# First features of xA issued on ScalarE's queue, and the softmax's 1e-9 as an addend of its sum

## The chip, the cores and the metric

The kernel runs on one core of a Trainium2 chip. The metric is the device time of one execution in microseconds (us). The engines are TensorE (PE, with its weight loads as PEld), VectorE (DVE), ScalarE (ACT), GpSimd (POOL) and SyncE (SP). SP and ACT can both issue DMA transfers; their issues appear as SPq and ACTq.

## The reference

The input x has 8 x 4096 tokens of 192 features. Eight heads of 24 features each have 7 taps; the taps go through a softmax with a small guard, and a causal convolution over the last 7 tokens follows. Its output goes through a dense layer to 2048, a squared ReLU with a scale and a bias, and a dense layer back to 192.

```python
w = np.exp(weight - np.max(weight, axis=-1, keepdims=True))
w = w / (np.sum(w, axis=-1, keepdims=True) + 1e-09)
x_pad = np.concatenate([np.zeros((B, pad, D)), x], axis=1)
idx = np.arange(S)[:, None] + np.arange(K)[None, :]
x_unf = x_pad[:, idx, :].reshape(B, S, K, H, group)
out = np.einsum('hk,bskhg->bshg', w, x_unf)        # then reshaped to tokens x 192
h = out @ w_in
g = s * np.maximum(h, 0.0) ** 2 + b
return g @ w_out
```

## The kernel before

Features lie on the partitions and tokens along the free axis. The 192 features are cut into A, the first 128, and B, the last 64, of which two blocks of 512 tokens are laid on top of each other so that B too fills 128 partitions. A step n takes 1024 tokens, that is two blocks j; there are 32 steps. The hidden 2048 are 8 pairs p of 2 x 128. Matrices are split into a high and a low fp32r part, and products are formed as high x high, high x low and low x high.

`Tokens.load` brings the tokens of a step: it clears the six padding columns of xA where a sequence begins (L133, on POOL), then issues xB (L135) and xA (L138) on SP. At n = 0 only the first 512 tokens of xA go with L138; then come the first third of the words of pair 0 (`fetch`, L338) and the rest of xA (L141).

The setup lies at the end of the pools: the taps' DMA (L345), `tok[0].load()`, an identity made on POOL, an Exp on ACT whose result nobody reads (L357; it has the activation table loaded early), and the softmax of the taps on DVE and ACT, L358 to L366: maximum, subtraction, Exp, sum, addition of 1e-9, reciprocal, product. More words and the two scalars follow on SP's queue.

`head` then does step 0's convolution: PE warms up on a tile of zeros (L382) and convolves both blocks of B at once into a PSUM tile with seven diagonal matrices that ACT makes from the taps (L390, L245); DVE convolves block 0 of A (L149 for the first tap, L151 for the six others); PE convolves block 1 of A (L245 again). Splits follow: ACT casts the sum to the high part (L166, L215), and the low part is a subtraction on DVE (L168) or, for the sums in PSUM, a matmul with minus the identity (L218) and a copy (L219). Weight words are split on ACT and DVE at L292 to L325. The first matmuls of the dense layer are at L526.

The order of DVE, ACT and PE is the order of the program text (`in_order`), and so is that of SP's queue in `head`. The rest is ordered by the recording layer, with the waits that data need; `behind(...)` holds an instruction back until the engine's last one so far has been issued.

Of the kernel before, what the change touches and what calls it, by code (L numbers as in the profile page):

```python
# [9 lines left out]
F32 = mybir.dt.float32  # L10
# [3 lines left out]
AF = mybir.ActivationFunctionType  # L14
ALU = mybir.AluOpType
AX = mybir.AxisListType

P = 128
# [17 lines left out]
def conv_attention_then_squared_relu_mlp(  # L36
# [23 lines left out]
    nc = tc.nc  # L60
    D, T = outT.shape
    NPAIR = weights64.shape[0]
    K = taps.shape[2]
    PAD = K - 1
# [5 lines left out]
    const = ctx.enter_context(tc.tile_pool(name="const", bufs=1))  # L70
# [10 lines left out]
    def last_of(*engines):  # L81


        traced = nc.cur_bb.bb.instructions
        last = [next(i for i in reversed(traced) if i.engine == e.engine) for e in engines]

        @contextmanager
        def context():
            with ExitStack() as stack:
                for i in last:  # L90
                    stack.enter_context(tc.issue_after(i))
                yield

        return context

    def behind(*engines):
        return last_of(*engines)()
# [20 lines left out]
    class Tokens:  # L118
# [7 lines left out]
        def load(self):  # L126
            n = self.n
            t0 = n * SUP
            self.xA = xin.tile([P, PAD + SUP], F32, name="xA")
            self.xB = xin.tile([P, PAD + BLK], F32, name="xB")  # L130
            skip = PAD if t0 % seq == 0 else 0
            if skip:
                nc.gpsimd.memset(self.xA[:, 0:PAD], 0.0)  # L133

            nc.sync.dma_start(self.xB, xB[n])  # L135
            x0 = t0 - PAD
            cut = PAD + BLK if n == 0 else PAD + SUP
            nc.sync.dma_start(self.xA[:, skip:cut], xA[:, x0 + skip : x0 + cut])  # L138
            if n == 0:
                fetch(0, 0, CI)  # L140
                nc.sync.dma_start(self.xA[:, cut:], xA[:, BLK:SUP])  # L141
# [192 lines left out]
    def fetch(p, a=0, z=None):  # L334
        if a == 0:
            words[p] = wordp.tile([P, CT, 2], I32, name="words")
        z = z or CT
        nc.sync.dma_start(  # L338
            words[p][:, a:z].rearrange("p f w -> p (f w)"), w_words[p, :, 2 * a : 2 * z]
        )  # L340

    idle = act.tile([P, 2, BLK], F32, name="q")[:, 0, 0:P]
    nc.gpsimd.memset(idle, 0.0)
    tap = const.tile([P, 2, K], F32, name="tap")
# [9 lines left out]
    tmax = const.tile([P, 2], F32, name="tmax")  # L354
    tsum = const.tile([P, 2], F32, name="tsum")

    nc.scalar.activation(tsum, idle[:, 0:2], AF.Exp)  # L357
    nc.vector.reduce_max(tmax, tap, axis=AX.X)  # L358
    nc.vector.tensor_tensor(
        tap, tap, tmax.unsqueeze(2).to_broadcast([P, 2, K]), op=ALU.subtract  # L360
    )
    nc.scalar.activation(tap, tap, AF.Exp)
    nc.vector.reduce_sum(tsum, tap, axis=AX.X)
    nc.vector.tensor_scalar(tsum, tsum, 1e-9, None, op0=ALU.add)
    nc.vector.reciprocal(tsum, tsum)
    nc.vector.tensor_tensor(tap, tap, tsum.unsqueeze(2).to_broadcast([P, 2, K]), op=ALU.mult)  # L366

    fetch(0, CI, CT)
    fetch(1)
# [474 lines left out]
```

## Time and profile before

| | us |
|---|---|
| median of 3 runs (2297.73 to 2298.25) | 2298.07 |
| the profiled execution | 2297.88 |
| its span, first to last instruction | 2296.1 |
| PE busy | 2289.9 |
| DVE busy | 1755.8 |
| ACT busy | 1287.5 |
| POOL busy | 317.0 |

The span is what the trace covers; the profiled execution's own time is 1.8 us longer. A row of the timeline gives the start from the span's beginning, the duration, the engine, the line of the kernel, the operation, output<-input, and in brackets how long the engine sat idle before it and what ended that. A DMA's issue is short; the time to its landing stands in the rows on DMA issues.

### The profile page before, as it was taken

The page shows a single profiled execution, that of the slowest core. Times are in us where ns is not written, and L with a number is a line of the kernel's source. Part 1 is how long each engine was busy: PE and PEld are TensorE (multiplying, and loading weights), DVE is VectorE, ACT ScalarE, POOL GpSimd, SP SyncE. Part 2 cuts the span into 40 slices and gives each one's busy share as a digit, 9 for nine tenths or more (in the row PEclk, how much of TensorE's full clock was granted, in tenths as well). Part 3 has the DMA queues.
Part 4 walks back from the last instruction along what each step waited for, and adds up shares of the span by engine and source line. Part 5 has one row for each costly group of instructions (what it writes and reads, how often), then busy time and mean ns, then how long its engine had stood idle before and what let it go on. Part 6 is the DMA issues. An engine that isn't in the chain of part 4 may idle for free.

```text
span 2296.1 us, 45081 instructions
## 1 busy us (share of the span) xinstructions
PE 2289.9 (100%) x19330; PEld 1829.1 (80%) x19330; DVE 1755.8 (76%) x1995; ACT 1287.5 (56%) x1410; POOL 317.0 (14%) x205
## 2 busy tenths in 40 slices
PE   9999999999999999999999999999999999999999
PEld 6788888888888888888888888888888888888887
DVE  8898777777777787777877777777777777777764
ACT  8755555555555556455555555555555555555554
POOL 0021101101111011110110111101101111011110
PEclk9999999999999999999999999999999999999999
DMA  5113112121121111111111212112121121111110
GB/s 175 38 40 86 42 38 61 49 54 42 43 56 51 51 42 50 49 52 52 44 49 47 55 49 53 47 40 60 49 54 43 43 56 51 51 43 43 42 38 17
DMA packets 46168, 117.51 MB, mean 51 GB/s; under 512 B 7760, under 2 KB 8016, under 8 KB 45968
## 3 DMA queue, kind: packets, MB, share of 16 engines
q1 hardware_dynamic: 45824, 114.50, 18.9%
q8 instruction: 151, 2.47, 0.5%
q14 instruction: 49, 0.40, 0.1%
q10 hardware_dynamic: 144, 0.13, 0.0%
HBM read 31.64 MB, written 25.17 MB: 25 GB/s over the span
## 4 chain that ended last, share of the span: by engine, by line
PE 99%; DVE 1%; DMA 0%; ACT 0%; SPq 0%; issue 0%; DVEq 0%
PE acc L609 50%; PE h L526 47%; PE acc L571 0%; PE acc L572 0%; PE acc L577 0%; PE acc L576 0%; PE acc L578 0%; DVE accA L151 0%; DMA xA<-in_xA 0%; DVE t L303 0%; DVE t L300 0%; DVE t L296 0%; DVE oB L671 0%; ACT W L310 0%; PE acc L668 0%
## 5 line engine op out<-in xcount | busy, mean ns | idle before, releaser
L540 ACT ACTIVATE q<-h 128x1024 f32<-128x1024 f32 x512 | 526.3, 1028 | 966.0 <-PE h L526 958.8
L549 DVE CAST qh<-q 128x1024 fp32r<-128x1024 f32 x497 | 372.8, 750 | 455.6 <-ACT q L547 454.6
L554 DVE TENSOR_TENSOR ql<-q,qh 128x1024 fp32r<-128x1024 f32 x512 | 656.7, 1283 | 56.9 <-ACT qh L549 3.3
L609 PE MATMUL acc<-qh,W 64*128 64x512 f32 x3960 | 622.0, 392 | 0.0
L547 ACT ACTIVATE q<-q 128x1024 f32<-128x1024 f32 x512 | 543.0, 1061 | 16.0
L609 PEld LDWEIGHTS acc<-qh,W 64*128 64x128 f32 x3960 | 370.9, 184 | 91.1
L526 PE MATMUL h<-sA,W 64*128 64x512 f32 x3072 | 441.8, 392 | 0.0
L526 PE MATMUL h<-wA,W 64*128 64x512 f32 x3072 | 441.2, 392 | 0.0
L526 PE MATMUL h<-tB,W 64*128 64x512 f32 x1536 | 439.6, 392 | 0.0
L526 PE MATMUL h<-wB,W 64*128 64x512 f32 x1536 | 439.6, 392 | 0.0
L609 PE MATMUL acc<-ql,WB 64*128 64x512 f32 x1980 | 391.2, 392 | 0.0
L609 PE MATMUL acc<-qh,WB 64*128 64x512 f32 x1980 | 391.1, 392 | 0.0
L609 PE MATMUL acc<-ql,W 64*128 64x512 f32 x1980 | 391.0, 392 | 0.0
L633 POOL TENSOR_TENSOR oB<-oB,oB 128x512 f32<-128x512 f32 x61 | 115.4, 1892 | 1731.7 <-ACT oB L632 1731.7
L151 DVE SCALAR_TENSOR_TENSOR accA<-xA,tap,accA 128x512 f32<-128x512 f32 x378 | 340.5, 901 | 6.8
L526 PEld LDWEIGHTS h<-sA,W 64*128 64x128 f32 x3072 | 287.3, 184 | 72.7 <-issue 1.5
L526 PEld LDWEIGHTS h<-wA,W 64*128 64x128 f32 x3072 | 287.7, 184 | 70.6
L526 PEld LDWEIGHTS h<-tB,W 64*128 64x128 f32 x1536 | 282.6, 184 | 47.1 <-issue 0.2
L526 PEld LDWEIGHTS h<-wB,W 64*128 64x128 f32 x1536 | 282.6, 184 | 23.7
L609 PEld LDWEIGHTS acc<-ql,WB 64*128 64x128 f32 x1980 | 185.5, 184 | 46.0 <-DVE ql L554 0.6
L609 PEld LDWEIGHTS acc<-ql,W 64*128 64x128 f32 x1980 | 185.5, 184 | 45.5
L609 PEld LDWEIGHTS acc<-qh,WB 64*128 64x128 f32 x1980 | 185.5, 184 | 45.4
(115 smaller groups left out, 1035.6 us busy)
## 6 DMA issues: line engine op xcount, KB each, us to landing
wA<-sA SPq DMA_DIRECT2D x126, 256.0 KB, 3.7
outT<-oA SPq DMA_DIRECT2D x63, 256.0 KB, 2.0
wB<-tB SPq DMA_DIRECT2D x60, 256.0 KB, 3.5
xA<-in_xA SPq DMA_DIRECT2D x24, 515.0 KB, 3.6
xB<-in_xB SPq DMA_DIRECT2D x32, 259.0 KB, 2.7
oC<-oB SPq DMA_DIRECT2D x61, 128.0 KB, 2.2
outT<-oC SPq DMA_DIRECT2D x60, 128.0 KB, 2.3
words<-in_w SPq DMA_DIRECT2D x7, 768.0 KB, 6.0
```

The source lines that it names most:

```text
L151: nc.vector.scalar_tensor_tensor(acc, src, w[:, k : k + 1], acc, op0=ALU.mult, op1=ALU.add)
L526: nc.tensor.matmul(h[:, i, :], w_in(w, p, chunk[0], rows), chunk[part], start=start, stop=stop)
L540: nc.scalar.activation(q, h, AF.Relu)
L547: nc.scalar.activation(q, q, AF.Square)
L549: cast(qh, q)
L554: nc.vector.tensor_tensor(ql, q, qh.bitcast(F32), op=ALU.subtract)
L609: nc.tensor.matmul(accs[to + 2 * i], w(f, r), q[r, f % 2, :], start=start and f == 0, stop=stop and f == ends[i],)
L633: nc.gpsimd.tensor_tensor(o[1], o[1], o[3], op=ALU.add)
```

## The change

At step 0 the first 512 tokens of xA are issued by ACT instead of SP, and POOL's memset of the padding covers eight columns instead of six, so that it overlaps the first two columns that the transfer writes. The unread Exp is held behind ACT's last instruction so far, which is that issue. In the softmax the Exp writes into a new tile `powers` of 8 columns per group, whose last column POOL sets to 1e-9; the sum runs over all eight, the separate addition is gone, and the product reads `powers`. Line numbers grow by 4 to 9.

```diff
             if skip:
-                nc.gpsimd.memset(self.xA[:, 0:PAD], 0.0)
-
+                nc.gpsimd.memset(self.xA[:, 0 : PAD + 2 * (n == 0)], 0.0)
             nc.sync.dma_start(self.xB, xB[n])
             x0 = t0 - PAD
             cut = PAD + BLK if n == 0 else PAD + SUP
-            nc.sync.dma_start(self.xA[:, skip:cut], xA[:, x0 + skip : x0 + cut])
+            (nc.sync if n else nc.scalar).dma_start(
+                self.xA[:, skip:cut], xA[:, x0 + skip : x0 + cut]
+            )
...
-    nc.scalar.activation(tsum, idle[:, 0:2], AF.Exp)
+    with behind(nc.scalar):
+        nc.scalar.activation(tsum, idle[:, 0:2], AF.Exp)
...
-    nc.scalar.activation(tap, tap, AF.Exp)
-    nc.vector.reduce_sum(tsum, tap, axis=AX.X)
-    nc.vector.tensor_scalar(tsum, tsum, 1e-9, None, op0=ALU.add)
+
+    powers = const.tile([P, 2, K + 1], F32, name="powers")
+    nc.gpsimd.memset(powers[:, :, K:], 1e-9)
+    nc.scalar.activation(powers[:, :, 0:K], tap, AF.Exp)
+    nc.vector.reduce_sum(tsum, powers, axis=AX.X)
     nc.vector.reciprocal(tsum, tsum)
-    nc.vector.tensor_tensor(tap, tap, tsum.unsqueeze(2).to_broadcast([P, 2, K]), op=ALU.mult)
+    nc.vector.tensor_tensor(
+        tap, powers[:, :, 0:K], tsum.unsqueeze(2).to_broadcast([P, 2, K]), op=ALU.mult
+    )
```

SP's queue before, from the program's beginning (tap: the taps; words: weight words; DMAHW is a DMA's semaphore):

```order
L345 DMA tap<-in_taps 128x14
L135 DMA xB<-in_xB 128x518
L138 DMA xA<-in_xA 128x512
L338 DMA words<-in_w 128x768
L141 DMA xA<-in_xA 128x512
L338 DMA words<-in_w 128x768
L338 DMA words<-in_w 128x1536
```

SP's queue in the changed kernel, the same place:

```order
L349 DMA tap<-in_taps 128x14
L137 DMA xB<-in_xB 128x518
L342 DMA words<-in_w 128x768
L145 DMA xA<-in_xA 128x512
L342 DMA words<-in_w 128x768
L342 DMA words<-in_w 128x1536
```

The third issue, the first part of xA, is gone, and all behind it stand one place further ahead.

ACT before, from its first instruction (q: at L357 the tile of zeros, at L390 a diagonal):

```order
L357 ACT_TABLE_LOAD
L357 ACTIVATE tsum<-q 128x2 [waits Pool_49]
L362 ACTIVATE tap<-tap 128x14 [waits DVE_49]
L390 ACTIVATE q<-q,tap 128x128 [waits DVE_49,Pool_49]
L390 ACTIVATE q<-q,tap 128x128 x6
```

ACT in the changed kernel, the same place:

```order
L140 DMA xA<-in_xA 128x512 [waits Pool_49]
L362 ACT_TABLE_LOAD
L362 ACTIVATE tsum<-q 128x2
L370 ACTIVATE powers<-tap 128x2x7 [waits DVE_49]
L399 ACTIVATE q<-q,tap 128x128 [waits DVE_49,Pool_49]
L399 ACTIVATE q<-q,tap 128x128 x6
```

The issue of xA is now ACT's first instruction and waits for POOL; the table load and the unread Exp come behind it.

## Rows read from the trace of the kernel before

**Rows 1.** The page's first part: engine, busy us, share of the span, instructions.
```profile
PE 2289.9 (100%) x19330; PEld 1829.1 (80%) x19330; DVE 1755.8 (76%) x1995; ACT 1287.5 (56%) x1410; POOL 317.0 (14%) x205
```
**Rows 2.** Waits of PE, whole run: tile, line, releaser, us, times, longest.
```profile
PE acc L382 <- POOL xA L133: 1.0, 1, 1.0
PE acc L218 <- ACT sA L215: 0.4, 1, 0.4
PE acc L218 <- ACT hiB L215: 0.2, 1, 0.2
```
**Rows 3.** The chain of waits, 0 to 60 us: start us, us, what.
```profile
0.74 0.40 SPq L345
...
1.19 0.42 SPq L135
...
1.65 3.26 DMA xA<-in_xA
...
18.16 0.49 ACT sA L215
...
18.70 0.50 PE acc L218
```
**Rows 4.** Timeline, 0 to 16 us, ACT, SP, DVE: start, us, instruction, [idle before <-releaser].
```profile
0.73 1.28 ACT L357 ACT_TABLE_LOAD   x1 [0.73 <-PEq L834]
...
2.13 0.43 SPq L338 DMA_DIRECT2D words<-in_w  x1
...
2.79 0.21 ACT L362 ACTIVATE tap<-tap 128x14 f32<-128x14 f32 x1 [0.57 <-DVE tap L359]
...
3.04 0.17 DVE L363 TENSOR_REDUCE tsum<-tap 128x2 f32<-128x14 f32 x1 [0.28 <-ACT tap L362]
...
3.24 0.17 DVE L364 TENSOR_SCALAR tsum<-tsum 128x2 f32<-128x2 f32 x1
...
3.65 0.17 DVE L366 TENSOR_TENSOR tap<-tap,tsum 128x14 f32<-128x14 f32 x1
3.92 2.15 ACT L390 ACTIVATE q<-q,tap 128x128 f32<-128x128 f32 x7 [0.91 <-DVE tap L366]
...
5.05 0.49 DVE L149 TENSOR_SCALAR accA<-xA,tap 128x512 f32<-128x512 f32 x1 [1.23 <-DMA xA<-in_xA]
```
**Rows 5.** Timeline, the memset of xA's padding on POOL.
```profile
0.87 0.10 POOL L133 MEMSET xA<- 128x6 f32 x1
```
**Rows 6.** Timeline, PE from its first matmul to 18.70 us.
```profile
0.99 3.43 PE L382 MATMUL acc<-q 128*128 128x512 f32 x6 [0.99 <-POOL xA L133]
...
4.38 6.28 PE L245 MATMUL acc<-xB,q 128*128 128x512 f32 x14
...
10.49 1.88 PE L245 MATMUL acc<-xA,q 128*128 128x512 f32 x4
...
12.60 0.50 PE L218 MATMUL acc<-hiB,minus 128*128 128x512 f32 x1 [0.23 <-ACT hiB L215]
...
18.70 0.50 PE L218 MATMUL acc<-sA,minus 128*128 128x512 f32 x1 [0.40 <-ACT sA L215]
```
**Rows 7.** DMA issues of 1.5 to 2.4 us: queue, count, KB each, us to landing.
```profile
xB<-in_xB SPq DMA_DIRECT2D x1, 259.0 KB, 2.9
xA<-in_xA SPq DMA_DIRECT2D x1, 256.0 KB, 3.3
...
words<-in_w SPq DMA_DIRECT2D x1, 384.0 KB, 4.2
```
**Rows 8.** Stretches: busy us (instructions) by engine; PE clock, DMA share, GB/s.
```profile
2.50:3.00 0.50, 0.50 (x2) 0.14 (x1) 0.23 (x2) 0.20 (x1) 0.00 (x0) 1.00 0.83 153
3.00:3.50 0.50, 0.50 (x3) 0.41 (x2) 0.39 (x3) 0.01 (x1) 0.00 (x0) 1.00 0.99 282
...
0.00:20.00 20.00, 18.37 (x50) 8.55 (x52) 15.41 (x32) 14.93 (x35) 0.88 (x8) 1.00 0.59 187
```
**Rows 9.** Timeline near the end: the one DMA issue on ACT's queue.
```profile
2292.20 0.38 ACTq L690 DMA_DIRECT2D outT<-oA  x1
```

## Prediction

> **What bounds the kernel now.** I read the engine totals first: TensorE (PE) is busy 2289.9 of 2296.1 us [rows 1]. So the kernel is one long stream of matmuls, and a change can move the end only by moving the moment that stream starts, or by opening a gap in it. The waits of PE over the whole run come next: 1.0, 0.4 and 0.2 us, all in the first 19 us [rows 2]. Behind them the stream has only small gaps that hang on its own results, so what the start gains is carried to the end one for one.
>
> Then I read the chain of waits of that start, from the first DMA to 18.70 us, where PE begins the stream that never pauses for long [rows 3]. In order: SP issues the taps (0.74) and xB (1.19), then xA, which runs from 1.65 to 4.92; VectorE (DVE) starts the convolution of block 0 with it at 5.05 and from there convolution and weight splitting follow each other on the chain without a pause; ScalarE (ACT) takes over, to the cast of sA at 18.16; PE's L218 at 18.70. DVE stood idle 1.23 us ahead of 5.05, waiting for xA [rows 4]. The softmax of the taps, which the same instruction needs, had ended at 3.65 + 0.17 = 3.82. So of the two things that the change touches, xA's landing is late by 1.23 us and the softmax is early by as much.
>
> **What is removed, added and moved.** *The issue of xA.* Before, it stands third on SP: the issues of taps and xB are ahead of it, each some 0.45 us from start to start (0.74, 1.19, 1.65) [rows 3]. After, it stands first on ACT and waits for one Pool memset, made two columns wider so that it overlaps the transfer. That memset starts at 0.87 and takes 0.10 [rows 5]; two more columns I cost at nothing. PE's first matmul, released by Pool too, starts at 0.99 [rows 6]. So the issue starts at about 1.03 (0.97, and 0.06 from the semaphore to a start), which is 0.62 earlier than 1.65 and 0.16 ahead of xB's own, which stays at 1.19.
>
> When does it land? Before, xB landed 2.9 us after its issue (4.1) and xA 3.3 after its own (4.92) [rows 7]: xA came 0.8 us behind xB, and 256 KB in 0.8 us is what the queue moved then, near the 282 GB/s of 3.0 to 3.5 us at a DMA share of 0.99 [rows 8]. The DMA engines were full; only below 3.0 us was there room (153 GB/s, share 0.83). So the pair cannot come much sooner than before: the last of both at 4.92 - 0.16 = 4.76. Which of them comes first is not in this trace: no row has two issuing queues at once. If xA is served whole, it lands at 1.03 + 2.9 = 3.93; if the two alternate, both at about 4.76. I take xA at 4.4, the middle and a little to the late side, and xB at 4.75. DVE then starts 0.13 after the landing (4.92 to 5.05), at 4.53: **0.52 us sooner**. The bounds are 3.93 (start 4.06, 0.99 sooner) and 4.76 (start 4.89, 0.16 sooner). Below nothing: three transfers, xB, xA and the 384 KB of words, may share the engines; the words, issued at 2.13 [rows 4], landed at 2.13 + 4.2 = 6.3 [rows 7] and are now issued 0.45 sooner, so 5.9 would be xA's worst, 0.97 us later than before.
>
> *xB pays for it.* PE's convolution of xB started at 4.38, some 0.3 after xB's landing, when ACT had made the first diagonal, begun at 3.92 [rows 4, 6]. With xB at 4.75 and some 0.06 from a semaphore to a start, it starts at 4.81: 0.43 later. PE has slack to lose. Its 14 passes for xB fill 4.38 to 10.49, 0.43 to 0.44 us each; the next four leave the array free at 10.49 + 4 x 0.43 = 12.21, and L218 started at 12.60, so 0.39 of waiting there (0.23 by the row, whose modelled ends include some drain: the four are 1.88 long and 1.72 by their spacing, 0.16 apart). The second L218, at 18.70, shows 0.40 idle, with the same drain about 0.56 [rows 6]. Together 0.95. PE can therefore bring 18.70 forward by 0.95 - 0.43 = 0.52 at most; DVE's 0.52 is just covered. Were xA first and DVE 0.99 sooner, PE would still hold the gain at about 0.5. That is why the forecast is flat over much of the unknown: a transfer that is served first lets DVE start, and the other one then limits PE.
>
> *ACT's table load.* It ran from 0.73 to 2.01, ahead of anything that needed it [rows 4]. Now it stands behind the issue, which takes 0.38 on ACT as the one such row shows [rows 9]: 1.03 + 0.38 + 0.04 = 1.45, load to 2.73, the warming Exp (0.2, as the real one) to 2.94, so the real Exp starts at 2.95 and not 2.79: 0.16 later. *The softmax's guard.* The addition at 3.24 goes, one step of 0.20 (3.04, 3.24) [rows 4]; the 1e-9 becomes an eighth element of the sum, written by a Pool memset that nobody waits for until 3.2. Sum +0.16 - 0.20 = -0.04: the taps are ready at 3.78, ACT's diagonals start as before. Cost nothing, under cover of the wait for xA; if xA landed at 3.93, its start at 4.06 would still be behind 3.78. Both bounds: if the issue held ACT for 0.6, the taps would be ready at 4.0, still under 4.53.
>
> *SP's other issues* (words, second half of xA, words) move up 0.45 each. The first words landed at 6.3 [rows 7], and no piece of the chain is one of these transfers [rows 3]: nothing is gained, and their bytes stand behind xB on SP's queue.
>
> **Sum.** The profiled execution took 2297.88 us, 1.8 over its span. With 0.52 less it is 2297.4; the median of the three runs stands 0.19 above the profiled one, at 2298.07, so I forecast 2298.07 - 0.5 = **2297.6 us**, a gain of 0.02%. What this kernel's measurement can tell from no change is about 0.2%, or 4.6 us: nine times the gain.
>
> **The rivals.** *It doesn't do what it says (no gain).* The two queues alternate evenly, xA and xB land together at 4.76, DVE starts 0.16 sooner; a little more loss in alternation makes it nought: 2298.0, within 0.3. For it: the engines were already full from 3.0 us. Against it: xA's lead of 0.16 and the room before 3.0. The Trainium skill, "DMA: Bandwidth & Descriptors", section "Issuing engines are not separate DMA queues", speaks for this one: DMAs of all issuing engines run on the same 16 DMA engines and interleave, and a second issuer saves only issue time. By that rule the gain would be 0.2 rather than 0.5; no row here shows it. Chance, by the shares and the lead above: 25%.
>
> *Both early.* The slow beginning (153 GB/s before 3.0) is waiting time that two queues overlap; then xA lands near 4.0 and xB near 4.3, DVE gains 0.9 and PE's slack of 0.95 is untouched: 2297.1. 12%.
>
> *xB becomes the bound (slower).* From a landing at 4.38 + 0.95 - 0.06 = 5.3 on, PE's convolution of xB sets 18.70, and each further 0.1 costs 0.1. With xB sharing with xA and the words until 5.9 that is 0.6: 2298.7. Against it: the words stand behind xB on the same queue. 6%.
>
> *The clock falls (much slower).* PE's warming matmuls end at 0.99 + 3.43 = 4.42 [rows 6]; a late xB leaves PE idle to 4.8. If the clock then fell from 2.4 to 1.2 GHz, the 14 passes of xB would take 0.86 and not 0.43 each, 6.0 us more, less the slack left (0.5): 2303.5. It decides when the idle stretch is longer than those that the granted clock survived; the 0.40 before 18.70 left it at 1.00 [rows 6, 8]. 2%.
>
> **How the numbers follow.** Forecast 55%, 2297.3 to 2297.8 by itself. The three runs before span 0.52 us, so each case is blurred by 0.3. The range reaches to "both early" below (2297.1 - 0.3) and to no gain above (2298.1 + 0.3): 2296.8 to 2298.4, leaving out the slower cases and the tails. Faster by over 0.2% would need 4.6 us at the start, and the whole wait for xA is 1.23: 1%. Slower by over 0.2% is the clock alone: 2%. The rest, 97%, is within.
>
> **What would show it.** xA issued on ACT near 1.03, the table load near 1.45, DVE's L149 (now L153) near 4.5 with its idle time still put down to xA; PE's first xB pass near 4.8, put down to xB and not to ACT; the idle time ahead of both L218 (now L222) shrunk to almost nothing; the long run of matmuls from near 18.2. Wrong if DVE starts at 4.9 or later, if the softmax ends after xA lands, or if PE's passes at 5 us stand more than 0.43 apart.

## The result and the profile after

The changed kernel took 2306.54 us (median of 6 runs, 2306.32 to 2307.54) where the kernel before took 2297.9 beside it: ratio 1.0038, interval 1.0027 to 1.0049. It is 8.6 us **slower**; the forecast was 0.5 us faster, with a range that ended at 2298.4.

The first part of the page after, to be read against [rows 1]:

```profile
PE 2299.7 (100%) x19330; PEld 1837.9 (80%) x19330; DVE 1754.8 (76%) x1994; ACT 1289.8 (56%) x1410; POOL 318.4 (14%) x206
```

PE's busy time grew by 9.8 us with the same 19330 matmuls; that of the other engines hardly moved. So the time did not come as a gap. PE's waits over the whole run after are fewer than in [rows 2]:

```profile
PE acc L391 <- POOL xA L136: 1.0, 1, 1.0
```

The start was no worse either. The timeline after, 0 to 20 us (columns as in [rows 4]):

```profile
1.01 0.38 ACTq L140 DMA_DIRECT2D xA<-in_xA  x1
...
1.42 1.28 ACT L362 ACT_TABLE_LOAD   x1 [1.42 <-POOL powers L369]
...
3.71 0.17 DVE L373 TENSOR_TENSOR tap<-powers,tsum 128x14 f32<-128x14 f32 x1
3.92 0.48 DVE L153 TENSOR_SCALAR accA<-xA,tap 128x512 f32<-128x512 f32 x1
3.98 2.15 ACT L399 ACTIVATE q<-q,tap 128x128 f32<-128x128 f32 x7 [0.79 <-DVE tap L373]
...
4.64 7.04 PE L249 MATMUL acc<-xB,q 128*128 128x512 f32 x14
...
11.51 1.88 PE L249 MATMUL acc<-xA,q 128*128 128x512 f32 x4
...
18.74 0.51 PE L222 MATMUL acc<-sA,minus 128*128 128x512 f32 x1
```

DVE starts 1.13 us sooner than in [rows 4] and no longer waits for xA. The second L222 (L218 before) starts at 18.74 against 18.70 in [rows 6], without its 0.40 of idle time. Up to there nothing is lost and nothing gained; the 8.6 us lie behind.

Where, a table by stage shows. One stretch of 400 us in the middle, before (engines as in [rows 8]: PE, PEld, DVE, ACT, POOL; behind the busy us, in brackets, how many instructions began):

```profile
400.00:800.00 400.00, 400.00 (x3432) 321.09 (x3430) 304.96 (x339) 219.55 (x236) 55.25 (x35) 1.00 0.19 50
```

and after:

```profile
400.00:800.00 400.00, 400.00 (x3418) 321.39 (x3416) 303.99 (x340) 219.11 (x235) 54.38 (x35) 1.00 0.18 50
```

PE is busy throughout in both, at a granted clock of 1.00, and gets 3418 matmuls done instead of 3432: 0.41% fewer, about as much as the whole run lost (0.38%). The stretches of 400 us behind it repeat it. The pace can also be read off the starts. Matmuls on 64 rows run in pairs, one on each half of the array. Before:

```profile
599.69 0.40 PE L609 MATMUL acc<-ql,WB 64*128 64x512 f32 x2
...
601.09 0.63 PE L609 MATMUL acc<-qh,W 64*128 64x512 f32 x4
```

after:

```profile
599.62 0.39 PE L618 MATMUL acc<-ql,WB 64*128 64x512 f32 x2
...
601.03 0.63 PE L618 MATMUL acc<-qh,W 64*128 64x512 f32 x4
```

Between these rows lie six pairs: 1.40 us before and 1.41 after. Over all pairs of 400 to 800 us the mean from start to start is 233.3 ns before and 234.3 after, in every group of matmuls, first and second layer alike. One nanosecond on each of some 9,700 pairs makes up the loss.

### The profile page after: what moved, and what is told of

It is laid out like the page before. It is cut to its first block, busy times and chain, and to the rows that moved or that the text cites. A ratio compares the mean times of both kernels' runs of the same rounds, so it can differ in the third digit from the quotient of the medians.

```text
span 2305.3 us, 45082 instructions
## 1 busy us (share of the span) xinstructions
PE 2299.7 (100%) x19330; PEld 1837.9 (80%) x19330; DVE 1754.8 (76%) x1994; ACT 1289.8 (56%) x1410; POOL 318.4 (14%) x206
## 4 chain that ended last, share of the span: by engine, by line
PE 100%; DVE 0%; DVEq 0%; issue 0%; POOL 0%; POOLq 0%
PE acc L618 50%; PE h L535 47%; PE acc L249 1%; PE acc L580 0%; PE acc L586 0%; PE acc L587 0%; PE acc L581 0%; PE acc L585 0%; PE acc L391 0%; DVE oB L680 0%; PE acc L677 0%; PE acc L222 0%; DVE oB L683 0%; DVEq L849 0%; PE acc L678 0%; DVE oA L696 0%
```

## The experiments

Two theories stood at first. **Layout:** the new tile `powers`, 64 bytes a partition, lies among the constants, and all tiles allocated behind it move by 64 bytes; PE's stream is slower for that. **Start:** the other start (an issue on ACT, a later rise of PE's clock) slows what follows. The program places W at byte 16512 of each partition, WB at 57472, and sA, the first tile of moving data, at 110560 before and 110624 after. WB lies a multiple of 256 from W, and sA, wA, tB, wB, qh and ql lie multiples of 256 from each other, so one number tells their place: the distance of moving data from weights within 256 bytes, 110560 - 16512 = 94048 = 367 x 256 + **96** before, **160** after.

### The change taken apart

**An unused tile of 64 bytes in the kernel before:**

```diff
     tsum = const.tile([P, 2], F32, name="tsum")
+    spare = const.tile([P, 2, K + 1], F32, name="spare")
+    nc.gpsimd.memset(spare[:, :, K:], 1e-9)
```

> The kernel before with one tile more in the constants: 64 bytes a partition, at the place where the change puts powers, two columns of it cleared by POOL and read by nobody. Nothing else is changed. Theory layout: the change is slow because the new tile moves every tile behind it by 64 bytes and PE's matmuls then stand 234.3 ns apart and not 233.3; this run is as slow as the changed kernel, 2306 to 2307 us. Theory start: the change is slow because of its other start (xA's issue on ACT, PE's clock rising late); this run is as the kernel before, 2298 us.

**The changed kernel with powers behind all other tiles:**

```diff
+    high = ctx.enter_context(tc.tile_pool(name="high", bufs=1))     # behind the last pool of SBUF
...
-    powers = const.tile([P, 2, K + 1], F32, name="powers")
+    powers = high.tile([P, 2, K + 1], F32, name="powers")
```

> The changed kernel with powers in a pool of its own behind all others, so that no other tile moves. Theory layout: 2297.5 to 2298.5 us, with 233.3 ns between matmuls. Theory start: 2306 to 2307 us, as the changed kernel.

**xA's issue alone** (the first and second piece of the change's diff, softmax as before):

> The kernel before with the first half of the change alone: xA's first part issued by ACT, the wider memset, the unread Exp behind the issue; softmax as before, no new tile. Theory layout: 2297.5 to 2298.5 us (DVE's first convolution near 4.1 us, but PE's start no earlier). Theory start: 2306 to 2307 us.

**The guard alone** (the last piece of the change's diff, xA on SP):

> The kernel before with the second half of the change alone: powers, the guard as an addend; xA issued by SP as before. Theory layout: 2306 to 2307 us, since powers moves the tiles behind it by 64 bytes. Theory start: 2298 us.

Measured, on one chip, the kernel before at 2297.8:

| run | us | ratio, interval | matmuls in 400 us |
|---|---|---|---|
| unused 64 bytes | 2307.19 | 1.0041 (1.0026 to 1.0056) | 3418 |
| powers behind all | 2297.78 | 0.9999 (0.9989 to 1.0009) | 3432 |
| issue alone | 2297.59 | 0.9999 (0.9990 to 1.0009) | 3432 |
| guard alone | 2307.26 | 1.0041 (1.0026 to 1.0056) | 3418 |

All four come out as layout had it and against start. 64 bytes that nobody reads cost all that the change cost, and the whole change without those 64 bytes in the way costs nothing.

### What about the place matters

**32 and 128 unused bytes instead of 64; 64 bytes ahead of the weights; 64 bytes ahead of qh and ql:**

```diff
+    spare = const.tile([P, 8], F32, name="spare")        # 32 bytes; [P, 32] for 128
...
+    spare = const.tile([P, 16], F32, name="spare")       # 64 bytes, ahead of W
     W = const.tile([P, NPAIR, 2, CB], F32R, name="W")
...
+    spare = gap.tile([P, 16], F32, name="spare")         # 64 bytes, ahead of the pool of qh and ql
```

> The kernel before with an unused tile of 32 bytes where the change puts powers: the tiles behind it (inputs, splits, activations) move by 32 bytes and begin at multiples of 128 bytes (before: 96 over one). Theory 128: what counts is the place of the matmuls' moving data within 128 bytes, 96 being good and 32 bad; a multiple may be as good or better, 2298 us or a little under. Theory any move: every place but the old one is worse, 2306 us.

> The same with 128 bytes: the tiles behind it again begin 96 over a multiple of 128 bytes. Theory 128: 2298 us, 233.3 ns between matmul pairs. Theory any move, or a place counted over more than 128 bytes: 2306 us.

> The same with 64 bytes ahead of the weights W, so that weights and moving data move together. Theory distance: what counts is the place of the moving data against that of the weights, which PE loads beside the stream; as before, 2298 us. Theory place: the moving data's own place counts; 2306 to 2307 us.

> The kernel before with 64 bytes between the activations q and the tiles qh and ql: only the moving data of the second layer (and the output tiles) move, sA, wA, tB, wB and q stay. Theory moving data: the pairs of the second layer stand 234.3 ns apart, those of the first layer 233.3; half of the loss and a little over, 2302 to 2303 us. Theory other engines (it is the tiles of DVE and ACT ahead of that place): 2298 us. Theory all or nothing: 2306 us.

The kernel before beside them took 2298.09. Measured: 32 bytes 2288.71 (ratio 0.9960, 0.9945 to 0.9975), faster than any run so far; 128 bytes 2297.80 (1.0000); 64 ahead of the weights 2297.85 (0.9999); 64 ahead of qh and ql 2304.96 (1.0030, 1.0019 to 1.0042). The stretch with 32 bytes:

```profile
400.00:800.00 400.00, 400.00 (x3446) 323.95 (x3444) 305.30 (x339) 219.38 (x236) 54.24 (x35) 1.00 0.18 50
```

With weights and moving data moved together, nothing changes: their distance counts, not where the moving data lies. "Any move is worse" falls with 32 bytes. The last run fits no theory cleanly. Half of the moving data moved, and most of the loss was there (6.9 of 9 us); the first layer's pairs slowed too, though neither their weights nor their data had moved. The matmuls of tB, 400 to 800 us, in the kernel before and in this run (behind the bar: busy us and mean ns of one):

```profile
L526 PE MATMUL h<-tB,W 64*128 64x512 f32 x270 | 77.2, 392 | 0.0
```
```profile
L529 PE MATMUL h<-tB,W 64*128 64x512 f32 x271 | 78.1, 394 | 0.0
```

From start to start its pairs went from 233.3 to 235.0 ns.

**PE by itself.** Is it PE's own reads, or the other engines' reads and writes in the same memory? From the fourth step on these kernels let PE repeat the same matmuls (38 to a pair of hidden groups, not the 36 of the first expectation) on the tiles that are there, with nothing beside it; they leave out the convolution, the activation and the output of those tokens:

```diff
-    NSUP = T // SUP
+    NSUP = 3
...
+    for n in range(3, T // SUP):
+        for j in range(2):
+            accs = [ps_o.tile([P, BLK], F32, name=f"acc{k}") for k in (1, 2, 1, 2)]
+            for p in range(NPAIR):
+                first(2, j, p)
+                stream(accs, p, qh, ql)
```

> The kernel before, which from the fourth step of 1024 tokens on computes nothing: PE alone repeats the 36 matmuls of a pair of hidden groups on the tiles that are there, with no convolution, activation, output or DMA beside it; the output of those tokens is missing. Read at 400 to 800 us. Theory PE's own reads: PE keeps the 233.3 ns from pair to pair that it has beside all the other work, since only its own reads of weights and moving data set it. Theory contention: the reads and writes of the other engines set it; alone PE is quicker, 232 ns or less, in this and the next two runs alike.

> The same with the 32 unused bytes. Theory PE's own reads: 232.4 ns, as in the full kernel with 32 bytes. Theory contention: the same as the run without them.

> The same with 64 unused bytes. Theory PE's own reads: 234.3 ns. Theory contention: the same as the run without them.

The same stretch without unused bytes, with 32 and with 64:

```profile
400.00:800.00 400.00, 400.00 (x3431) 321.05 (x3430) 0.00 (x0) 0.00 (x0) 0.00 (x0) 1.00 0.00 1
```
```profile
400.00:800.00 400.00, 400.00 (x3446) 323.95 (x3444) 0.00 (x0) 0.00 (x0) 0.00 (x0) 1.00 0.00 1
```
```profile
400.00:800.00 400.00, 400.00 (x3418) 321.21 (x3416) 0.00 (x0) 0.00 (x0) 0.00 (x0) 1.00 0.00 1
```

DVE, ACT and POOL at 0.00, DMA at 1 GB/s, and PE keeps 3431, 3446 and 3418, the counts of the full kernels (one execution each: 2294.1, 2285.0 and 2303.2 us). PE's own reads set its pace; contention with the other engines and with DMA falls.

**The changed kernel at a better place.** A longer `powers` moves the rest by 160 bytes:

```diff
-    powers = const.tile([P, 2, K + 1], F32, name="powers")
+    powers = const.tile([P, 5, K + 1], F32, name="powers")[:, 0:2, :]
```

> The changed kernel with powers 160 bytes long instead of 64 (three groups of eight unused), which moves the tiles behind it to multiples of 128 bytes. What 32 bytes did to the kernel before should hold here: 2288 to 2289 us, 0.4% under the kernel before, with 232.4 ns from pair to pair. If powers itself did harm by another way than its length: over 2298 us.

It took **2235.1 us** where the kernel before took 2297.88 (ratio 0.9726, 0.9712 to 0.9739): 2.7% faster and not the expected 0.4%. This is the version that beats both kernels. Its page:

```profile
PE 2227.3 (100%) x19330; PEld 1834.8 (82%) x19330; DVE 1753.4 (79%) x1994; ACT 1286.1 (58%) x1410; POOL 317.1 (14%) x206
```

and the stretch:

```profile
400.00:800.00 400.00, 400.00 (x3532) 331.45 (x3530) 314.14 (x348) 227.50 (x246) 59.73 (x38) 1.00 0.19 51
```

3532 against 3432 matmuls, 226.7 ns from pair to pair. I had counted places within 128 bytes, where 32 and 160 are the same; they are not. With 160 bytes the distance from the weights is 94208, a whole multiple of 256 (and of 4096). Four more runs take that apart.

```diff
+    spare = const.tile([P, 40], F32, name="spare")       # 160 bytes; [P, 104] for 416
...
+    ahead = const.tile([P, 8], F32, name="ahead")        # 32 bytes ahead of W, with 128 behind
     W = const.tile([P, NPAIR, 2, CB], F32R, name="W")
...
+    gap0 = gap.tile([P, 120], F32, name="gap0")          # 480 bytes ahead of qh and ql, with 160
```

> The kernel before with 160 unused bytes where the change puts powers, and nothing else of the change. Theory distance: what counts is the distance of PE's moving data from its weights within some power of two; it is now a multiple of 4096, so 2235 us as the changed kernel with 160 bytes, 226.7 ns from pair to pair. Theory both: the gain of the last run needs the change's other half too; 2288 to 2298 us.

> The same with 416 = 160 + 256 bytes. Theory 256: distances count within 256 bytes; 2235 us. Theory 512: they count within 512 or more; something else, 2288 to 2307 us.

> 32 unused bytes ahead of the weights W and 128 behind: the moving data lies at the very addresses of the run with 160 bytes, the weights 32 bytes further, so that the distance is that of the run with 128 bytes. Theory distance: 2298 us. Theory place of the moving data: 2235 us.

> 160 unused bytes as before, and 480 more ahead of qh and ql, so that only the first layer's moving data (sA, wA, tB, wB) lies at the good distance and the second layer's where 128 bytes put it. Theory each by itself: pairs of the first layer 226.7 ns apart, those of the second 233.3; 2268 us (2298 less 18 of 38 pairs' share of 63 us). Theory all or nothing, as the mixed run of qh and ql alone suggests: 2290 us or more.

Beside the kernel before at 2298.07: 160 bytes alone 2234.95 (ratio 0.9725, 0.9711 to 0.9740); 416 bytes 2234.85 (0.9725, 0.9710 to 0.9739); 32 ahead and 128 behind 2297.95 (0.9999); the first layer alone at the good distance 2279.21 (0.9918, 0.9903 to 0.9933). So the gain needs nothing of the change. 256 bytes further the same place comes again. And with the moving data at the very addresses of the 2235 us run but the weights 32 bytes on, it is gone: distance, within 256 bytes.

The last of the four by groups, 400 to 800 us (matmuls by line and operands, then busy us and mean ns of one):

```profile
L614 PE MATMUL acc<-qh,W 64*128 64x512 f32 x728 | 114.5, 392 | 0.0
L531 PE MATMUL h<-sA,W 64*128 64x512 f32 x548 | 78.1, 389 | 0.0
...
L531 PE MATMUL h<-wA,W 64*128 64x512 f32 x546 | 76.7, 386 | 0.0
```

In the first layer sA's matmuls come first and wA's last. The second layer stays at 392; after it sA's take 389, and wA's reach the 386 of the best run. A pair's pace depends on its own distance and, for some pairs, on what stood ahead of it. From start to start the first layer's pairs took 229.0 ns in the mean where 226.7 was expected; over its some 4,600 pairs that is the 11 us by which this run missed its expected 2268. It bears on the mixed run of qh and ql above too.

**How wide is the good place?** Two last runs, 96 and 192 unused bytes at the same spot:

> The kernel before with 96 unused bytes where the change puts powers: the moving data lies 192 over a multiple of 256 bytes from the weights. Theory only a whole multiple is good: 2288 to 2307 us, 232.4 ns or more from pair to pair. Theory the nearer the better: between 2235 and 2298 us, since 192 is 64 short of a multiple.

> The same with 192 unused bytes, 32 over a multiple. Theory only a whole multiple is good: 2288 to 2307 us. Theory the nearer the better: nearer to 2235 than the run with 96 bytes.

2297.83 (0.9999) and 2297.89 (1.0000) beside 2297.93. Of the distances tried only a whole multiple gives the 2.7%. 32 bytes to either side of it nothing is left, and 128 gives 0.4%. All distances tried, with the unused bytes that make them (those of the change and of the guard alone come under 160):

| distance within 256 | unused bytes | matmuls in 400 us | us |
|---|---|---|---|
| 0 | 160, 416 | 3534, 3532 | 2234.95, 2234.85 |
| 32 | 192 | 3432 | 2297.89 |
| 96 | none | 3432 | 2298.07 |
| 128 | 32 | 3446 | 2288.71 |
| 160 | 64 | 3418 | 2307.19 |
| 192 | 96 | 3430 | 2297.83 |
| 224 | 128 | 3432 | 2297.80 |

Untried is 64.

## Why the prediction was wrong

**The step that failed** is the first: "a change can move the end only by moving the moment that stream starts, or by opening a gap in it." It left out a third way, the pace of the stream itself. So the list of what is added held the instructions on `powers` and not the tile, and the guard was costed at nothing by its instructions, which was right for them; its 64 bytes cost 9 us. None of the rivals had it, and the clock, my one way to a slow stream, stood at 1.00. The page of the kernel before had a hint: a matmul of 64 x 512 took 392 ns in every group, PE was busy without a break, and nothing told whether that pace was the engine's or the layout's.

**xA's landing** was mis-sized. The issue at 1.03 was right (1.01). The rows of DMA issues after, to be read against [rows 7]:

```profile
xB<-in_xB SPq DMA_DIRECT2D x1, 259.0 KB, 3.3
xA<-in_xA ACTq DMA_DIRECT2D x1, 256.0 KB, 2.8
```

xA landed at 1.01 + 2.8 = 3.8, a little under the lower bound of 3.93, and xB at 1.19 + 3.3 = 4.5. The pair was done 0.4 us sooner than before; "the pair cannot come much sooner" allowed 0.16. The stretches after show the transfers under way sooner, against 59, 153 and 282 GB/s in the same three before (the last two in [rows 8]):

```profile
2.00:2.50 0.50, 0.50 (x2) 0.34 (x1) 0.11 (x1) 0.22 (x2) 0.00 (x0) 1.00 0.53 59
```
```profile
2.00:2.50 0.50, 0.50 (x2) 0.34 (x1) 0.00 (x0) 0.50 (x1) 0.00 (x0) 1.00 0.95 132
2.50:3.00 0.50, 0.50 (x2) 0.14 (x1) 0.34 (x2) 0.42 (x3) 0.00 (x0) 1.00 0.70 225
3.00:3.50 0.50, 0.50 (x3) 0.41 (x2) 0.17 (x1) 0.20 (x1) 0.00 (x0) 1.00 1.02 346
```

(the first fence is before, the second after). By the landings this is nearest to the rival "both early", which had 12%. But it takes no gain from a second queue to explain it. The sum moved the pair's end by the 0.16 of its first issue; the last of its two issues moved from 1.65 to 1.19, by 0.46, and the pair was done 0.42 sooner. The Trainium skill says of a second issuer that it saves only issue time ("DMA: Bandwidth & Descriptors", "Issuing engines are not separate DMA queues"). The trace agrees, with 0.42 us against the 0.46. Nor is the 0.42 firm: over all traces of this case the later of the two landed at 4.6 to 5.1 us in the sixteen with both on SP, and at 4.4 to 4.8 in the four with xA on ACT.

**The softmax** came out 0.1 us later than summed: ready at 3.71 + 0.17 = 3.88 and not 3.78. It was then DVE's bound, at 3.92; a softmax that ends after xA's landing is one of the prediction's signs against itself. Which of the two comes last is close: in the run with powers behind all others the taps were ready at 3.53 + 0.17 = 3.70, and DVE waited for xA until 4.00.

**PE's slack** was right in kind: PE took over the bound, and DVE's gain of 1.13 us stopped there. But xB took the smaller part of the slack. The 14 passes, 4.64 to 11.51, took 0.49 us each where 0.43 was costed, which the prediction had named as a sign against it. The tile's rows, before and after (durations min/median/max in ns):

```profile
L245 PE MATMUL acc<-xB,q x14: 590/592/697, 4.4 to 10.1; 128*128 128x512 f32 x14
```
```profile
L249 PE MATMUL acc<-xB,q x14: 590/592/1193, 4.6 to 11.1; 128*128 128x512 f32 x14
```

The slowest pass after took 1193 ns, twice the median of 592: the lower of the clock's two levels, 1.2 GHz, lasted into the convolution. The trace's first entry of the granted clock, at 1.00, stands at 3.9 us before and at 6.2 us after; ahead of it the stretches' column shows 1.00 only because nothing is recorded there. With the start 0.26 later (4.64 for 4.38, right behind xB's landing at 4.50) and 6.87 us instead of 6.11 for the 14 passes, PE gave up 1.0 us, all of its slack of 0.95; xB's share of it is at most the 0.26. The run with the issue alone shows the forecast's own case, with passes at full pace (4.96 to 11.05) and the second L220 at 18.29, 0.41 sooner than before:

```profile
4.96 6.25 PE L247 MATMUL acc<-xB,q 128*128 128x512 f32 x14 [0.19 <-ACT q L393]
11.05 1.88 PE L247 MATMUL acc<-xA,q 128*128 128x512 f32 x4
...
18.29 0.51 PE L220 MATMUL acc<-sA,minus 128*128 128x512 f32 x1
```

The later rise of the clock does not need the change. The kernel before with 32 unused bytes, with xA on SP and its old softmax, has it too:

```profile
L245 PE MATMUL acc<-xB,q x14: 590/592/1094, 4.6 to 11.0; 128*128 128x512 f32 x14
```

So have the runs with 160 unused bytes alone (slowest pass 1122 ns) and with PE by itself and no unused bytes (1174). It differs from one execution to the next; whether the change makes it more frequent, these runs don't tell. In the times, 2297.59 and 2297.78 against 2297.8, the start's 0.4 us cannot be seen either way, as the prediction said.

## What to carry to other kernels

A tile that is added is a change to every tile allocated behind it: list its bytes beside its instructions, and keep it behind the tiles that PE reads. Where PE is busy from end to end, compare how many matmuls it gets done in the same stretch before looking for gaps. In a kernel like this one, matmuls of 64 rows with a weight load each, try placing the moving data a whole multiple of 256 bytes from the weights; here an unused tile of 160 bytes was worth 2.7%, more than a hundred times what the change set out to win.

## What the hardware showed that I had not expected

- PE's pace depends on the distance of its moving data from its weights, within 256 bytes: 226.7 ns from pair to pair at 0, 232.4 at 128, 234.3 at 160, and 233.3 at 32, 96, 192 and 224. That PE's reads of the next weights get in the way of the moving data's would explain it; it is argued and not shown, since no run took the weight loads away.
- A pair's pace also hangs on the pairs ahead of it: first-layer matmuls at the good distance took 389 ns at first and 386 some pairs later. By what the earlier ones reach them is open, and so is why moving only qh and ql slowed the first layer.
- With xA issued on ACT's queue beside xB on SP's, xA landed at 3.8 to 4.2 us in four traces, against 4.6 to 5.1 in the sixteen with both in a row on SP. xB paid for it, with 4.4 to 4.8 against 3.9 to 4.2. The later of the two came 0.24 us sooner in the mean, less than the 0.46 by which the last issue moved.
- The granted clock of 1.00 sets in anywhere from 3.9 to 6.9 us in the traces that record it, with the same six warming matmuls ahead of it. The 14 passes of xB behind them took 6.0 to 7.2 us, so the start of one profiled execution can be 1 us off by that alone.
